# Queries projected transposed, and VectorE's 32x32 block transposes in place of TensorE's, in a linear-attention and gated-MLP layer

## The chip, the cores and the metric

The kernel runs on one core of one Trainium2 chip. The metric is the device time of one execution in microseconds (us). The engines are TensorE (PE in the profile, with its weight loads as PEld), VectorE (DVE), ScalarE (ACT), GpSimd (POOL) and SyncE (SP), which issues most DMAs. TensorE's granted clock was 1.00 over the whole profiled execution.

## What is computed

All numbers are float32. `x` has 2048 tokens of 512 features, there are 32 heads of 16 features, and the MLP is 1376 wide.

```python
xn = _layernorm(x)
q, k, v = split_heads(xn @ wqkv)                   # 32 heads of 16
pq, pk = q @ w_phi[h], k @ w_phi[h]                # per head
phi_q = concat(softmax(pq), softmax(-pq))          # 32 features per head
phi_k = concat(softmax(pk), softmax(-pk))
kv = phi_k^T v;  z = sum over tokens of phi_k      # per head
o = (phi_q kv) / (phi_q z + 1e-6)
s = o @ wo
g = silu(((xn W_gate) * (gate > 0) * (xn W_up)) W_down)
out = x + s * g
```

## The kernel before

Every product is made of three matmuls of float32r operands: high part by high part and the two mixed products (`mm3`, L188). `split` (L183) makes the two parts: ScalarE copies the high part, VectorE or GpSimd subtracts it for the low part.

The work has these stages:

1. *Token stage* (about 20 to 169 us). A loop over 16 tiles of 128 tokens (L910). The order alternates between two blocks of 512 tokens (`order`, L209: blocks 2 and 3 first, then 0 and 1). Each round normalizes a tile, turns it by four TensorE transposes (`turn`, L304) into the shared tile `XT` (or `a21` for one quarter of the odd tiles, L289), and projects keys, values and queries by 12 matmuls of 512 columns each (`project`, L346). `query` (L351) projects queries with the tokens on the partitions, copies the result to SBUF (`pqs`) and stores it in DRAM. The weights of keys and queries are first multiplied by `w_phi` (`fold`, L226). `features` makes phi_k, and `kv_products` accumulates kv in PSUM (`pkv`, 8 matmuls of 256 columns for each tile).
2. *MLP, in two halves* of 1024 tokens (L1042). For each of 11 slices of 128 MLP features, `gate_up` (L508) makes 7 groups of 6 matmuls of 512 columns (`pa` to `pd`), and `down` adds the down projection (`py`) for slices in chunks. The slices' weights are split in the first half (`f_prep`), one slice ahead, and stored in DRAM for the second.
3. *Queries*, beside the MLP. `q_pair` (L611) handles two tiles of 128 tokens: it loads `pq`, copies it to PSUM on ScalarE (`fetch`), takes maxima and minima, subtracts, applies exp, sums, weighs by z (`weigh`, on GpSimd, `zB` holds z for all 1024 columns) and normalizes; all with tokens on the partitions. `q_back` (L708) turns the normalized features `eq` by 16 TensorE transposes in four groups (`ppT`, L722), splits each group (`pTh` on ScalarE, `pTl` on VectorE, L723), and multiplies by kv (`pnum`, 16 matmuls of 256 columns). ScalarE copies the result to `o`, and four DMAs for each half store it (`o_store`). Pairs 0 to 2 belong to the first half, 3 to 7 to the second (`QUERIES`, L31).
4. *Output* after each half (L1104): `o_load` reads o (a load, and a GpSimd DMA that adds the second part), `o_split` splits it, `out_tile` (L781) makes 12 matmuls (`pso`), multiplies by the MLP's result, adds x and stores.

The order of instructions is fixed when the program is built. `Clock` (L56) is a planner: it keeps a modelled time for each engine (`FIXED` and `RATE` in cycles of TensorE, L59), and `pump` (L126), called between matmul groups, lets waiting jobs issue their next step when the model says that its inputs are ready and the engine is not too far behind. A step on TensorE or SyncE waits until its inputs have been ready for `MARGIN`, 3000 cycles. Each engine, and SyncE's queue, then runs its own list in that order.

```python
if key in ("tensor", "sync"):
    return all(self.there(x) + self.MARGIN <= self.now for x in tiles)
free = max(self.free[key], self.now)
return free - self.now <= self.LIMIT[key] * limit and all(self.there(x) <= free + 300 for x in tiles)
```

All engine instructions are recorded by one helper, so the profile gives L52 for them; the tiles' names tell them apart.

Of the kernel before, what the change touches and what calls it, by code (L numbers as in the profile page):

```python
# [13 lines left out]
P = 128  # L14
# [41 lines left out]
class Clock:  # L56
# [41 lines left out]
    def add(self, gen, after=0, limit=1):  # L98
        self.work.append([self.now + after * BT, (None,), gen, limit])
        return gen  # L100

    def later(self, after, op):
# [5 lines left out]
    def when(self, tile, op):  # L108
        def gen():
            yield "sync", tile  # L110
            op()
            yield None,
        self.add(gen())

    def due(self, at, wants, limit):
        key, *tiles = wants
# [32 lines left out]
def layer_kernel(ctx: ExitStack, tc: tile.TileContext, x, wkT, wqT, wv, wo, wf, cst, out):  # L149
# [52 lines left out]
    def flat(e):  # L202
        return e.rearrange("p h s f -> p (h s f)")
# [16 lines left out]
    def w_tile(name):  # L220
        return [(u2((P, D), f"{name}h", F32R), u2((P, D), f"{name}l", F32R)) for k in range(KD)]

    def rows(w):
        return lambda k: w[k]

    def fold(w, raw, k):  # L226

        p = ps(name="pfold")
        for j in range(KD):
            nc.tensor.matmul(p[:, j * P:(j + 1) * P], raw[:, j * P:(j + 1) * P], bd_sb[:, j, :],  # L230
                             start=True, stop=True)
        return lambda: split(*w[k], p)


    XT = sb.tile([P, 7, 2, 2, BT], F32R, tag="XT", name="XT")
    pace.shared = XT.name
    A21, XN, XF, SF = {}, {}, {}, {}

    def norm_stats(n):
        xt = X.pop(n)  # L240
# [43 lines left out]
    def xt_parts(n, s):  # L284

        if n % 2 == 0:
            return [(XT[:, A11:A12 + 1, s, :, cols(n)], slice(0, 2))]
        if n not in A21:
            A21[n] = u2((P, 2, 2, P), "a21", F32R)  # L289
        return [(A21[n][:, s], 0), (XT[:, A22, s, :, cols(n)], 1)]  # L290

    def hi_xt(n, p):
# [53 lines left out]
    def project(n, w, name):  # L346
        p = ps(name=name)
        mm3(p, xt_cols(n), rows(w), range(KD))
        return p

    def query(n):  # L351
        pq = project(n, WQ, "pq")
        t = u2((P, D), "pqs")
        nc.scalar.activation(t, pq, AF.Copy)
        b, i = order[n]
        PQ[b * TPB + i] = dram((P, D), f"pq{b * TPB + i}")
        pace.when(t, lambda: nc.sync.dma_start(PQ[b * TPB + i], t))

    def features(n, pk, pv, between):

# [239 lines left out]
            yield  # L600


    PQS, OD = {}, {}

    def q_load(q):
        for j in range(2):
            t = 2 * q + j
            PQS[t] = u2((P, D), "pql")
            nc.sync.dma_start(PQS[t], PQ[t])

    def q_pair(q):  # L611
        es = []
# [19 lines left out]

        def weigh(j):
            ez.append(u4((P, 1024), "ez"))
            nc.gpsimd.tensor_tensor(ez[j], flat(es[j]), zB, op=ALU.mult)

        def total(s, j):
            src = ez[j].rearrange("p (h f) -> p h f", f=DH) if s else groups(es[j])
# [6 lines left out]
        def expo(j):  # L645
            nc.scalar.activation(flat(es[j]), flat(es[j]), AF.Exp)

        yield "scalar", PQS[2 * q]
        fetch(0)
        yield "vector", pv[0]  # L650
        bounds(0)
        yield from step_of(q - 1, 2)
        yield "vector", pv[0]
        shift(0)
        yield "scalar", es[0], PQS[2 * q + 1]
        expo(0)
        fetch(1)
        yield "vector", pv[1]
        bounds(1)
        yield from step_of(q - 1, 4)  # L660
        yield "vector", pv[1]
        shift(1)
        if q + 1 < NP:
            q_load(q + 1)
# [5 lines left out]
        total(0, 0)  # L670
        yield "vector", es[1]
        total(0, 1)
        yield from step_of(q - 1, 5)
        yield "gpsimd", es[1]
        weigh(1)
        yield "vector", sums
# [15 lines left out]
        for j in range(2):  # L692
            yield "vector", r
            normalize(j)
        DONE_Q[q] = 0
        BACK[q] = pace.add(q_back(q, es))

    BACK, DONE_Q = {}, {}
# [9 lines left out]
    def q_back(q, es):  # L708


        OD[q] = dram((P, 4, 256), f"od{q}"), dram((P, 4, 256), f"ol{q}")
        ts = [(u4((P, 4, 256), "pTh", F32R), u4((P, 4, 256), "pTl", F32R)) for hf in range(2)]
        for j in range(2):
            for hf in range(2):
                th, tl = ts[hf]
                yield "vector", es[j]
                yield "tensor", es[j]
                ef = flat(es[j])
                p = ps((P, 4, P), name="ppT")
# [4 lines left out]
                if hf:  # L724
                    es[j] = None
                DONE_Q[q] += 1
        for hf in range(2):
            th, tl = ts[hf]
            yield "tensor", tl
            os_ = u4((P, 2, 2, 256), "o")  # L730
            for o in range(2):
                p = ps((P, 2, 256), name="pnum")
                for s in range(2):
                    g = 2 * o + s
                    mm(p[:, s, :], kvhl[:, 1, hf * 4 + g, :], th[:, g, :], True, False)
                    mm(p[:, s, :], kvhl[:, 0, hf * 4 + g, :], tl[:, g, :], False, True)
                nc.scalar.activation(os_[:, o], p, AF.Copy)
            ts[hf] = None
            DONE_Q[q] += 1
            pace.when(os_, lambda hf=hf, os_=os_: o_store(q, hf, os_))  # L740
        yield None,

    def o_store(q, hf, os_):

        for s in range(2):
            for part in range(2):
                r = slice(0, 64) if s == part else slice(64, P)
                to = slice(0, 64) if s == 0 else slice(64, P)
                nc.sync.dma_start(OD[q][part][to, 2 * hf:2 * hf + 2, :], os_[r, :, s, :])


    OHL, OF, SX, YK = {}, {}, {}, {}
# [53 lines left out]

    def wo_fetch(k):
        WR[k] = u2((P, D), "wor")
        nc.sync.dma_start(WR[k], wo[:, k, :])

    def wo_prep(k):
        raw, hi, lo = WR.pop(k), u2((P, D), "woh", F32R), u2((P, D), "wol", F32R)
# [43 lines left out]
    WK, WV, WQ = w_tile("wk"), w_tile("wv"), w_tile("wq")  # L856

    def wv_split(k):
        split(*WV[k], wv_raw[:, k, :], nc.gpsimd)
    norm_vector(0)  # L860
    folds = [fold(WK, wk_raw[:, k, :], k) for k in range(2)]
    norm_vector_apply(0)
# [110 lines left out]
    def state():  # L973
# [31 lines left out]
                low(g2 - 1)  # L1005
            yield "tensor", kvacc
        low(g2)
        zB = u4((P, 1024), "zB")
        for c in range(2):
            yield "tensor", zacc  # L1010
            p = ps(name="pz")
            nc.tensor.matmul(p, ones, flat(zacc)[:, c * 512:(c + 1) * 512], start=True, stop=True)
            nc.vector.tensor_copy(zB[:, c * 512:(c + 1) * 512], p)

    def all_queries(half):
        if not half:
# [25 lines left out]
    for half in range(2):  # L1042
        b0, b1 = 2 * half, 2 * half + 1
        for f in range(NF):
# [124 lines left out]
```

## Time and profile before

| | |
|---|---|
| time, median of 3 runs | 583.93 us (583.33 to 584.82) |
| the profiled execution's own time | 583.24 us |
| its span | 581.5 us |
| instructions | 8525 |
| busy: PE, DVE, ACT, POOL | 99%, 68%, 50%, 67% of the span |
| TensorE transposes of query features (`ppT`) | 128, 272 ns each |
| query projection (`pq`) | 192 matmuls of 128x512, about 390 ns each |
| numerators (`pnum`) | 128 matmuls of 128x256, about 280 ns each |
| DVE low parts (`pTl`) | 32 of 128x512, 690 ns each |
| POOL weighing (`ez`) | 16 of 128x1024, 2408 ns each |
| DMA | 138.26 MB, 238 GB/s on average |

The span runs from the first to the last instruction that the profiler recorded; the execution's own time is 1.7 us longer. In the profile's groups, a line names engine, operation, output<-inputs, shape and count, then the busy time of the group, the mean duration of one, and the idle time of the engine before them with what ended it. Matmuls overlap one another, so the duration of one is longer than its share of TensorE's time. The chain of waits follows the work that ended last back to its start, at each step to what released it. In the view of stretches, each engine has its busy time and, in brackets, its number of instructions.

### The profile page before, as it was taken

The page shows a single profiled execution, that of the slowest core. Times are in us where ns is not written, and L with a number is a line of the kernel's source. Part 1 is how long each engine was busy: PE and PEld are TensorE (multiplying, and loading weights), DVE is VectorE, ACT ScalarE, POOL GpSimd, SP SyncE. Part 2 cuts the span into 40 slices and gives each one's busy share as a digit, 9 for nine tenths or more (in the row PEclk, how much of TensorE's full clock was granted, in tenths as well). Part 3 has the DMA queues.
Part 4 walks back from the last instruction along what each step waited for, and adds up shares of the span by engine and source line. Part 5 has one row for each costly group of instructions (what it writes and reads, how often), then busy time and mean ns, then how long its engine had stood idle before and what let it go on. Part 6 is the DMA issues. An engine that isn't in the chain of part 4 may idle for free.

```text
span 581.5 us, 8525 instructions
## 1 busy us (share of the span) xinstructions
PE 575.2 (99%) x2786; PEld 480.2 (83%) x2786; DVE 395.6 (68%) x605; ACT 289.4 (50%) x529; POOL 390.1 (67%) x341
## 2 busy tenths in 40 slices
PE   8999999999999999999999999999999999999997
PEld 7788888888888888888888888888888888888886
DVE  4898777767648975888784532588888878673322
ACT  3998787854535358254244151144544545434510
POOL 1779988979875586997967342543557575775384
PEclk9999999999999999999999999999999999999999
DMA  8356999964698747888858999894676384769863
GB/s 309 128 173 173 270 291 264 296 183 100 194 262 298 287 149 234 288 290 285 274 201 260 330 392 397 314 388 161 162 252 167 128 248 151 194 206 276 247 176 114
DMA packets 82700, 138.26 MB, mean 238 GB/s; under 512 B 7648, under 2 KB 30560, under 8 KB 81760
## 3 DMA queue, kind: packets, MB, share of 16 engines
q1 hardware_dynamic: 79200, 125.60, 64.2%
q0 software_dynamic: 3312, 12.06, 10.8%
q8 instruction: 22, 0.36, 0.3%
q14 instruction: 22, 0.18, 0.1%
q10 hardware_dynamic: 144, 0.07, 0.0%
HBM read 77.14 MB, written 52.69 MB: 223 GB/s over the span
## 4 chain that ended last, share of the span: by engine, by line
PE 97%; DMA 1%; ACT 1%; DVE 1%; SPq 0%; issue 0%; POOL 0%; POOLq 0%
PE py L52 21%; PE pd L52 10%; PE pa L52 10%; PE pc L52 10%; PE pso L52 8%; PE pk L52 8%; PE pq L52 8%; PE pv L52 7%; PE pb L52 5%; PE pkv L52 3%; PE pnum L52 3%; PE ppT L52 2%; PE pxT L52 1%; PE pfold L52 1%; DMA wkT<-wkT 1%; PE pkb L52 0%
## 5 line engine op out<-in xcount | busy, mean ns | idle before, releaser
L52 PE MATMUL pa<-XT,wa 128*128 128x512 f32 x264 | 68.9, 393 | 0.0
L52 PE MATMUL py<-fdh,hl 128*128 128x512 f32 x176 | 68.8, 391 | 0.0
L52 PE MATMUL py<-fdh,hh 128*128 128x512 f32 x176 | 68.6, 390 | 0.0
L52 PE MATMUL py<-fdl,hh 128*128 128x512 f32 x176 | 68.5, 389 | 0.0
L52 POOL TENSOR_TENSOR hl<-e,hh 128x512 fp32r<-128x512 f32 x22 | 28.4, 1292 | 56.1 <-ACT hh L52 51.8
L52 PEld LDWEIGHTS pa<-XT,wa 128*128 128x128 f32 x264 | 48.5, 188 | 9.4
L52 ACT ACTIVATE hh<-e 128x512 fp32r<-128x512 f32 x22 | 13.9, 632 | 72.0 <-DVE e L52 65.0
L52 POOL TENSOR_TENSOR phl<-ek,phl 128x1024 fp32r<-128x1024 f32 x15 | 36.1, 2405 | 19.2 <-ACT phl L52 19.2
L52 POOL TENSOR_TENSOR hl<-u,hh 128x512 fp32r<-128x512 f32 x22 | 28.5, 1294 | 27.1 <-ACT hh L52 27.1
L52 DVE TENSOR_TENSOR y<-py,y 128x512 f32<-128x512 f32 x40 | 27.5, 689 | 27.2 <-PE py L52 27.1
L52 POOL TENSOR_TENSOR y<-y,ys 128x512 f32<-128x512 f32 x24 | 31.0, 1295 | 17.0 <-ACT ys L52 17.0
L52 PEld LDWEIGHTS py<-fdh,hh 128*128 128x128 f32 x176 | 33.0, 188 | 7.0
L52 PEld LDWEIGHTS py<-fdl,hh 128*128 128x128 f32 x176 | 33.1, 188 | 6.7
L52 PEld LDWEIGHTS py<-fdh,hl 128*128 128x128 f32 x176 | 33.0, 188 | 6.7
L52 POOL TENSOR_TENSOR ez<-eq,zB 128x1024 f32<-128x1024 f32 x16 | 38.5, 2408 | 0.0
L52 DVE TENSOR_TENSOR pTl<-ppT,pTh 128x512 fp32r<-128x512 f32 x32 | 22.1, 690 | 23.1 <-ACT pTh L52 22.7
L52 PE MATMUL pd<-XT,wd 128*128 128x512 f32 x132 | 35.0, 395 | 0.0
L52 POOL TENSOR_TENSOR ol<-of,oh 128x1024 fp32r<-128x1024 f32 x8 | 19.4, 2433 | 23.0 <-ACT oh L52 16.1
L52 PE MATMUL pd<-XT,wc 128*128 128x512 f32 x132 | 34.5, 392 | 0.0
L52 PE MATMUL pb<-XT,wb 128*128 128x512 f32 x132 | 34.5, 393 | 0.0
L52 PE MATMUL pc<-XT,wb 128*128 128x512 f32 x132 | 34.3, 391 | 0.0
L52 PE MATMUL pc<-XT,wc 128*128 128x512 f32 x132 | 34.1, 391 | 0.0
(166 smaller groups left out, 1637.6 us busy)
## 6 DMA issues: line engine op xcount, KB each, us to landing
zacc<-ek POOLq DMA_DIRECT2D x15, 512.0 KB, 5.2
xts<-XT SPq DMA_DIRECT2D x4, 1792.0 KB, 11.7
XT<-xts SPq DMA_DIRECT2D x7, 1024.0 KB, 14.9
wa<-ws SPq DMA_DIRECT2D x26, 256.0 KB, 5.3
wb<-ws SPq DMA_DIRECT2D x26, 256.0 KB, 5.2
wc<-ws SPq DMA_DIRECT2D x26, 256.0 KB, 5.3
rawg<-wf SPq DMA_DIRECT2D x22, 256.0 KB, 3.6
ws<-wa SPq DMA_DIRECT2D x22, 256.0 KB, 4.1
```

What stands on the lines that cost most here:

```text
L52: return self.tc.keep_in_program_order(op(*a, **k))
```

## The change

- *Projection.* `query` makes the queries with features on the partitions: the weights' slices of 128 columns are the stationary operand, two token tiles (256 columns) the moving one; 24 matmuls of 256 columns for each call instead of 12 of 512. The odd tiles' `a21` is shared by two tiles for that. The pair of tiles is the same that `q_pair` uses later.
- *To tokens.* `fetch` turns the loaded queries by a VectorE transpose of 32x32 blocks into PSUM, instead of ScalarE's copy. A partition then holds one of 32 tokens and one of four groups of features; the rest of both lies in the free dimension.
- *To features.* `q_back` turns `eq` by a VectorE block transpose into the tile of `ez`, instead of 16 TensorE transposes; ScalarE makes the high part of 1024 columns, and VectorE (pairs 0 to 2) or GpSimd (pairs 3 to 7) the low part. `pnum` reads its moving operand in runs of 32 columns. The result goes into the tile of `eq`.
- *Heads.* Keys, values and the rows of `wo` are taken with even heads first, by views where their weights are split or loaded. `zB` has 256 columns and is broadcast over the token blocks.
- *Order.* `q_back` goes to the front of the planner's list; the waits between pairs (`step_of`) are fewer; the second half's queries start after 5 matmul times instead of 30; an output tile's store waits until the planner holds it for ready, instead of 10 matmul times; `o_load` waits for the issue of its stores. There are 10 u4 buffers instead of 9 and 41 u2 instead of 44.

```diff
-B8, B4, B2 = 3, 9, 44
+B8, B4, B2 = 3, 10, 41
...
+        self.work.insert(0 if first else len(self.work), [self.now + after * BT, (None,), gen, limit])
...
+    def even_first(t):
+        return t.rearrange("p (m a f) -> p a m f", a=2, f=DH)
+    def by_parity(t):
+        return t.rearrange("p (a m f) -> p a m f", a=2, f=DH)
...
     def query(n):
-        pq = project(n, WQ, "pq")
-        t = u2((P, D), "pqs")
-        nc.scalar.activation(t, pq, AF.Copy)
...
+        b, h, j = order[n - n % 4 + n % 4 // 2][0], n // 4, n % 2
+        c = slice(h % 2 * 2 * P, (h % 2 + 1) * 2 * P)
...
+        p = ps((P, 2, 2 * P), name="pq")
+        for d in range(2):
+            w = slice((2 * j + d) * P, (2 * j + d + 1) * P)
+            mm3(p[:, d, :], lambda k: [t[:, w] for t in WQ[k]], x_of, range(KD))
...
         def fetch(j):
             pv.append(ps(name="pq2"))
-            nc.scalar.activation(pv[j], PQS.pop(2 * q + j), AF.Copy)
+            t = PQS.pop(2 * q + j)
+            nc.vector.transpose(pv[j], t.rearrange("p d t -> p (d t)"))
...
+            z = zB[:, 2 * j:2 * j + 2, :].unsqueeze(2).to_broadcast([P, 2, 8, 64])
...
-        BACK[q] = pace.add(q_back(q, es))
+        BACK[q] = pace.add(q_back(q, es, ez), first=True)
...
-                for g in range(4):
-                    c = (hf * 4 + g) * P
-                    transpose(p[:, g, :], ef[:, c:c + P])
-                split(th[:, :, j * P:(j + 1) * P], tl[:, :, j * P:(j + 1) * P], p)
...
+            et, ez[j] = ez[j], None
+            nc.vector.transpose(et, flat(es[j]))
...
+            nc.scalar.activation(th, et, AF.Copy)
+            lo = "vector" if q in QUERIES[0] else "gpsimd"
+            yield lo, th
+            add(getattr(nc, lo), tl, et, f32(th), ALU.subtract)
...
+            vh, vl = (t.rearrange("p (d t a x) -> p d a t x", d=2, a=2, x=32) for t in (th, tl))
...
+                    mm(o, kvhl[:, 1, g, :], vh[:, s, a], True, False)
+                    mm(o, kvhl[:, 0, g, :], vl[:, s, a], False, True)
...
     def o_load(q):
         pace.finish(BACK[q])
+        for g in STORES.pop(q):
+            pace.finish(g)
...
-            pace.later(10, lambda: nc.sync.dma_start(to, y))
+            pace.when(y, lambda: nc.sync.dma_start(to, y))
...
+        a, j = divmod(k, 2)
+        for s in range(2):
+            nc.sync.dma_start(WR[k][64 * s:64 * s + 64, :],
+                              wo[:, 2 * j + s, :].rearrange("(i a f) d -> a i f d", a=2, f=DH)[a])
...
-                queries = pace.add(all_queries(1), 30)
+                queries = pace.add(all_queries(1), 5)
```

More of the change, by code (lines that the diff above doesn't have):

```diff
@@ L96, in issued, with add @@
         self.ready[o.name] = self.free[key] + (380 if key == "tensor" else 0)
-    def add(self, gen, after=0, limit=1):
-        self.work.append([self.now + after * BT, (None,), gen, limit])
+    def add(self, gen, after=0, limit=1, first=False):
+        self.work.insert(0 if first else len(self.work), [self.now + after * BT, (None,), gen, limit])
         return gen
@@ L112, in gen @@
             yield None,
-        self.add(gen())
+        return self.add(gen())
     def due(self, at, wants, limit):
@@ L231, in fold @@
                              start=True, stop=True)
-        return lambda: split(*w[k], p)
+        if w is WQ:
+            return lambda: split(*w[k], p)
+        return lambda: split(*map(by_parity, w[k]), even_first(p))
     XT = sb.tile([P, 7, 2, 2, BT], F32R, tag="XT", name="XT")
     pace.shared = XT.name
-    A21, XN, XF, SF = {}, {}, {}, {}
+    A21, A21P, XN, XF, SF = {}, {}, {}, {}, {}
     def norm_stats(n):
@@ L288, in xt_parts @@
         if n not in A21:
-            A21[n] = u2((P, 2, 2, P), "a21", F32R)
+            if n % 4 == 1:
+                A21P[n // 4] = u4((P, 2, 2, 2 * P), "a21", F32R)
+            c = n // 2 % 2 * P
+            A21[n] = A21P[n // 4][:, :, :, c:c + P]
         return [(A21[n][:, s], 0), (XT[:, A22, s, :, cols(n)], 1)]
@@ L351, in query, with x_of @@
     def query(n):
-        pq = project(n, WQ, "pq")
-        t = u2((P, D), "pqs")
-        nc.scalar.activation(t, pq, AF.Copy)
-        b, i = order[n]
-        PQ[b * TPB + i] = dram((P, D), f"pq{b * TPB + i}")
-        pace.when(t, lambda: nc.sync.dma_start(PQ[b * TPB + i], t))
+        b, h, j = order[n - n % 4 + n % 4 // 2][0], n // 4, n % 2
+        c = slice(h % 2 * 2 * P, (h % 2 + 1) * 2 * P)
+        def x_of(k):
+            if n % 4 < 2:
+                return XT[:, k // 2, 0, k % 2, c], XT[:, k // 2, 1, k % 2, c]
+            if k // 2:
+                return XT[:, A22, 0, k % 2, c], XT[:, A22, 1, k % 2, c]
+            return A21P[h][:, 0, k, :], A21P[h][:, 1, k, :]
+        p = ps((P, 2, 2 * P), name="pq")
+        for d in range(2):
+            w = slice((2 * j + d) * P, (2 * j + d + 1) * P)
+            mm3(p[:, d, :], lambda k: [t[:, w] for t in WQ[k]], x_of, range(KD))
+        if n % 4 == 3:
+            A21P.pop(h)
+        t = u2((P, 2, 2 * P), "pqs")
+        nc.scalar.activation(t, p, AF.Copy)
+        q = 2 * b + h % 2
+        PQ[q, j] = dram((P, 2, 2 * P), f"pq{q}{j}")
+        pace.when(t, lambda: nc.sync.dma_start(PQ[q, j], t))
     def features(n, pk, pv, between):
@@ L606, in q_load @@
         for j in range(2):
-            t = 2 * q + j
-            PQS[t] = u2((P, D), "pql")
-            nc.sync.dma_start(PQS[t], PQ[t])
+            PQS[2 * q + j] = u2((P, 2, 2 * P), "pql")
+            nc.sync.dma_start(PQS[2 * q + j], PQ[q, j])
     def q_pair(q):
@@ L646, in expo @@
             nc.scalar.activation(flat(es[j]), flat(es[j]), AF.Exp)
-        yield "scalar", PQS[2 * q]
+        yield from step_of(q - 2, 4)
+        yield "vector", PQS[2 * q]
         fetch(0)
@@ L651, in q_pair @@
         bounds(0)
-        yield from step_of(q - 1, 2)
-        yield "vector", pv[0]
         shift(0)
-        yield "scalar", es[0], PQS[2 * q + 1]
+        yield "scalar", es[0]
         expo(0)
+        yield "vector", PQS[2 * q + 1]
         fetch(1)
@@ L659, in q_pair @@
         bounds(1)
-        yield from step_of(q - 1, 4)
-        yield "vector", pv[1]
         shift(1)
@@ L672, in q_pair @@
         total(0, 1)
-        yield from step_of(q - 1, 5)
         yield "gpsimd", es[1]
@@ L694, in q_pair @@
             normalize(j)
-        DONE_Q[q] = 0
-        BACK[q] = pace.add(q_back(q, es))
-    BACK, DONE_Q = {}, {}
+        DONE_Q[q], STORES[q] = 0, []
+        BACK[q] = pace.add(q_back(q, es, ez), first=True)
+    BACK, DONE_Q, STORES = {}, {}, {}
     def step_of(q, k):
@@ L706, in step_of, with q_back @@
                 yield 1,
-    def q_back(q, es):
+    def q_back(q, es, ez):
         OD[q] = dram((P, 4, 256), f"od{q}"), dram((P, 4, 256), f"ol{q}")
-        ts = [(u4((P, 4, 256), "pTh", F32R), u4((P, 4, 256), "pTl", F32R)) for hf in range(2)]
         for j in range(2):
[L714 to L719, printed above, removed]
-                for g in range(4):
-                    c = (hf * 4 + g) * P
-                    transpose(p[:, g, :], ef[:, c:c + P])
-                split(th[:, :, j * P:(j + 1) * P], tl[:, :, j * P:(j + 1) * P], p)
[L724 to L728, printed above, removed]
+            yield "vector", es[j]
+            et, ez[j] = ez[j], None
+            nc.vector.transpose(et, flat(es[j]))
+            DONE_Q[q] += 1
+            th, tl = u4((P, 1024), "pTh", F32R), u4((P, 1024), "pTl", F32R)
+            yield "scalar", et
+            nc.scalar.activation(th, et, AF.Copy)
+            lo = "vector" if q in QUERIES[0] else "gpsimd"
+            yield lo, th
+            add(getattr(nc, lo), tl, et, f32(th), ALU.subtract)
+            del et
@@ L729, in q_back @@
             yield "tensor", tl
-            os_ = u4((P, 2, 2, 256), "o")
-            for o in range(2):
+            os_ = flat(es[j]).rearrange("p (a s t) -> p a s t", a=2, s=2)
+            vh, vl = (t.rearrange("p (d t a x) -> p d a t x", d=2, a=2, x=32) for t in (th, tl))
+            for a in range(2):
                 p = ps((P, 2, 256), name="pnum")
                 for s in range(2):
[L734 to L737, printed above, removed]
@@ L738, in q_back @@
-            ts[hf] = None
+                    g = 4 * a + 2 * j + s
+                    o = p[:, s, :].rearrange("p (t x) -> p t x", x=32)
+                    mm(o, kvhl[:, 1, g, :], vh[:, s, a], True, False)
+                    mm(o, kvhl[:, 0, g, :], vl[:, s, a], False, True)
+                nc.scalar.activation(os_[:, a], p, AF.Copy)
+            es[j] = None
+            del th, tl, vh, vl
             DONE_Q[q] += 1
-            pace.when(os_, lambda hf=hf, os_=os_: o_store(q, hf, os_))
+            STORES[q].append(pace.when(os_, lambda j=j, os_=os_: o_store(q, j, os_)))
@@ L741, in q_back, with o_store @@
         yield None,
-    def o_store(q, hf, os_):
+    def o_store(q, j, os_):
         for s in range(2):
@@ L748, in o_store @@
                 to = slice(0, 64) if s == 0 else slice(64, P)
-                nc.sync.dma_start(OD[q][part][to, 2 * hf:2 * hf + 2, :], os_[r, :, s, :])
+                nc.sync.dma_start(OD[q][part][to, j:4:2, :], os_[r, :, s, :])
     OHL, OF, SX, YK = {}, {}, {}, {}
@@ L1007, in state @@
         low(g2)
-        zB = u4((P, 1024), "zB")
-        for c in range(2):
+        zB = small(256, "zB", 1).rearrange("p (d x) -> p d x", d=4)
+        for a in range(2):
             yield "tensor", zacc
-            p = ps(name="pz")
-            nc.tensor.matmul(p, ones, flat(zacc)[:, c * 512:(c + 1) * 512], start=True, stop=True)
-            nc.vector.tensor_copy(zB[:, c * 512:(c + 1) * 512], p)
+            p = ps((P, 4, 4, 32), name="pz")
+            nc.tensor.matmul(p.rearrange("p d i x -> p (d i x)"), ones, flat(zacc)[:, a * 512:(a + 1) * 512],
+                             start=True, stop=True)
+            for i in range(4):
+                r = slice(32 * i, 32 * i + 32)
+                nc.scalar.activation(zB[r, :, 32 * a:32 * a + 32], p[r, :, i, :], AF.Copy)
     def all_queries(half):
```

6 lines of the change are left out of this document (3 added, 3 removed).

## The prediction

> **What bounds the kernel now.** I read the page first: busy times, then the chain that ended last.
>
> ```profile
> span 581.5 us, 8525 instructions
> ...
> PE 575.2 (99%) x2786; PEld 480.2 (83%) x2786; DVE 395.6 (68%) x605; ACT 289.4 (50%) x529; POOL 390.1 (67%) x341
> ...
> PE 97%; DMA 1%; ACT 1%; DVE 1%; SPq 0%; issue 0%; POOL 0%; POOLq 0%
> ```
>
> The chain is TensorE's (PE) own list, one matmul after the other. The view of PE's waits asks whether anybody makes it wait:
>
> ```profile
> PE pidle L52 <- DVE mhalf L52: 1.1, 1, 1.1
> PE pfold L52 <- DMA wkT<-wkT: 0.9, 1, 0.9
> PE pv L52 <- POOL wvl L52: 0.5, 2, 0.3
> PE pxT L52 <- DVE lr L52: 0.2, 1, 0.2
> ```
>
> 2.7 us, all in the first 23 us. So what leaves PE's list leaves the time, one for one, as long as nobody new makes PE wait. What an instruction costs in that list is its pitch, not its duration. The chain between 208 and 228 us gives pitches:
>
> ```profile
> 212.13 1.37 PE py L52 x6
> 213.49 0.44 PE ppT L52 x4
> 213.93 1.39 PE pd L52 x6
> ```
>
> Six matmuls of 512 columns take 1.37 us (0.227 each) though one lasts 0.39; four transposes take 0.44, though one lasts 0.272.
>
> **The change, part by part** (own time of the profiled execution: 583.24 us, span 581.5).
>
> 1. *Transposes leave PE.* `ppT` is 128 instructions, 32 groups of four: 32 x 0.44 = 14.1 us. The piece behind a group takes 1.39 instead of 1.36 or 1.37 (pd above, also pb, pc): about 0.015 to 0.03 x 32, another 0.5. Together **-14.6**; without any of the slow start behind a group it would be 32 x 0.353 = 11.3 (three pitches of 0.108 and one short one of 0.028, read from the starts at 209.46).
>  The Trainium skill (TensorE: Matmul & The Clock Gate, Part 4: PE-mode transpose) gives about 275 ns for one such transpose in a kernel. The trace agrees as to the duration (272), but an estimate by that figure, 128 x 0.275 = 35 us for this part, is refuted by the pitch; the sum does not use it.
>
> 2. *Query projection.* 192 matmuls of 512 columns (43.7 us by pitch) become 384 of 256 columns, with twice the weight loads. The nearest row is `pkv`: 128x256, new weights each time, 128 of them in 15.1 us from start to start, 0.118 each. 384 x 0.1175 = 45.1: **+1.4**. Bounds: 0 (half of 0.227 each) and +28.5, if each weight load of 188 ns were paid in full (384 x 0.188 - 43.7); I take pkv, whose loads also last 188 and are hidden, and that speaks against the upper end so plainly that the range leaves it out. The pair of token tiles that a query now needs: for query(0) tile 2's low part on VectorE (DVE) ended at 26.4 us and pq began at 28.9, so 2.5 us of cover; later pairs have a whole round of 9.3 us.
>
> 3. *pnum* stays 128 matmuls of 256 columns (pitch 0.117), but reads its moving operand in runs of 32 columns. No row shows such a read. Bounds 0 and +14 (the pitch of 512 columns); I take 0, since what pnum shares with all rows is one column per pitch step.
>
> 4. *VectorE work.* Per query pair come two transposes of 512 and two of 1024 columns; four `pTl` of 0.69 go; for pairs 0 to 2 two low parts of 1024 come to DVE, for pairs 3 to 7 to GpSimd (POOL). No row shows a DVE transpose. Nearest are DVE operations of that size: 0.69 (`eq<-pq,mx`) and 1.21 (`eq<-eq,qr`); from below 0.55 (`xn` of 512 elements, all in SBUF), from above twice the size, 1.4 and 2.4. I take 0.69 and 1.21.
>  The stretches of the queries, before (busy columns PE, PEld, DVE, ACT, POOL):
>
> ```profile
> 195.00:309.00 114.00, 114.00 (x551) 95.37 (x550) 89.61 (x131) 52.59 (x101) 92.12 (x88) 1.00 0.72 237
> 375.00:533.00 158.00, 158.00 (x775) 132.24 (x774) 122.97 (x175) 77.74 (x132) 94.78 (x67) 1.00 0.68 215
> ```
>
>  First half: DVE +3 x 3.5 = 100 us in 114 - 12 x 0.44 = 108.7, 92% (from above, with transposes twice as long, 98%). POOL 92 of 108.7. Second half: DVE +5 x 1.0 = 128 in 149.2 (86%), POOL +10 x 2.41 = 119 (80%). All fit, the first half narrowly. ACT loses 9.4 (`pq<-pql`) and some of `pTh`: no cover needed. The weighing by a broadcast `zB` keeps 2.41; strided POOL rows of that size (`phl`, 2.405) show no surcharge; from above 3.1 (twice 1.54, `XT<-sa`), which is 16 x 0.7 on POOL.
>
> 5. *What is late next.* Before, DVE's normalizing released `ppT`, and `pTl` released `pnum`; the planner leaves 3000 of its cycles (1.25 us) ahead of a PE step, and in the trace the last pTl ended 1.0 to 2.2 us ahead of the second half's pnum (0.97 at 497.25, 1.43 at 227.24). After, three steps in a row stand there: DVE transpose, ACT high part, low part. They are modelled 3 to 9% short (1024 columns: DVE 1.09 against 1.13 pitch, ACT 0.87 against 0.95), 0.3 us in all. And the low part on DVE reads two SBUF tiles, which the kernel avoided so far for large tiles (its factor lies in PSUM). The few small ones show the price:
>
> ```profile
> 421.45 0.29 DVE L52 TENSOR_TENSOR qs<-qs,qr 128x128 f32<-128x128 f32 x1
> 421.77 1.32 DVE L52 SCALAR_TENSOR_TENSOR qd<-qs 128x64 f32<-128x64 f32 x1
> ```
> ```profile
> 421.72 1.29 POOL L52 TENSOR_TENSOR hl<-u,hh 128x512 fp32r<-128x512 f32 x1 [2.27 <-ACT hh L52]
> ```
>
>  `qd` takes 0.22 when POOL is idle and here 1.32, until POOL's instruction ends. So each of the six low parts of pairs 0 to 2 can wait 0 to 2.4 us for a POOL instruction, about 1.0 on average with POOL at 85%, and hold POOL 1.2 us itself. Against 1.0 to 1.6 of cover that leaves some 0.3 us of PE wait each, 1.8, and 0.3 for the ten POOL low parts: **+2.1** (bounds 0 and 16 groups x 1.5 = 24).
>  The Trainium skill (GPSIMD Engine Reference, section 8, Key points) states that GpSimd shares its SBUF interfaces with VectorE, in contention where a VectorE instruction has two SBUF inputs or a 2-port mode. The trace agrees (1.32 for 0.22). Whether a transpose from SBUF to SBUF falls under it, no run here shows.
>
> 6. *The last pair.* In the changed order the second half of pair 7's pnum stands 27 matmuls (6.1 us) ahead of the first `pso`, where before it stood in the last gate-and-up block. Behind it: ACT 1.1, four stores 2.6 and landing 2.4, load 3.6 (548.85 to 552.48), POOL accumulation behind yk, yk and ol (about 560.1 instead of 555.9), landing 7.6 (555.9 to 563.5), oh 1.05, ol 2.4: about 571.6, and tile 14 begins at 572.1. Cover 0.5; I take **+0.5** (bounds 0 and +4).
>
> 7. *The tail.* Stores of the output wait until the planner holds y for ready, no longer ten matmuls. Thus on SyncE's queue both half stores of tile 15 now stand ahead of those of tiles 12, 13 and 14, which before were issued earlier but for one between the halves:
>
> ```profile
> 577.40 1.72 SPq L52 DMA_DIRECT2D out<-y  x3
> ```
>
>  Three issues in 1.72 with waits; 577.40 and 577.83 stand back to back, 0.43 each; the 512-wide one landed 2.1 us after issue, the last half 1.7. Three more: 3 x 0.43 + 0.4 = **+1.7** (bounds 0 and 2.5).
>
> Nothing else moves PE: stores and loads of pq, the wo rows (two DMAs instead of one, four times) and zB are as long as before and off the chain; 10 u4 and 41 u2 buffers serve fewer live tiles per pair.
>
> Sum: 583.2 - 14.6 + 1.4 + 2.1 + 0.5 + 1.7 = 574.3 for the profiled execution. The median shown, 583.93, lies 0.7 above it: **575.0**.
>
> **The rivals.**
> - *All cover holds, and the tail does not grow*: without 2.1, 0.5 and 1.7 it is 570.0 + 0.7 = 570.7; with the tail 572.4. For it: DVE is below 93%. Against: the order of the stores is fixed in the program.
> - *The first half fills up*: transposes last twice as long or hold for POOL too. DVE at 98% plus six holds of 1.0 is 104%: some 4 to 8 us more of PE wait, 579 to 583.
> - *Slower*: pnum takes the wait. If each of the 16 groups has its low part 2.5 us late (the big transpose held like `xn`, which took 1.50 at 13.19 us under a POOL instruction instead of 0.55, and then the low part again, behind a weighing of 2.41), then 1.25 us of cover leave 1.25 x 16 = 20 in place of 2.1: 593. It decides from 11.0 us of waits on, 0.69 per group, where the gain is gone. Against: in pairs 3 to 7 no DVE operation of size has two SBUF tensors. (Point 3 at its upper end would give 589.)
> - *It doesn't do what it says*: the order lists have no ppT, 32 VectorE transposes and 384 pq. Excluded.
>
> **How the numbers follow.** Forecast with waits between 0 and 6 us (572 to 579): 0.62. Clean, below 572: 0.13. First half full, 579 to 582.2: 0.12. Around the old time, within 0.3% (1.75 us, about what a measurement can tell from no change): 0.06. Slower: 0.07. Faster: 0.87. The range leaves out what lies below 571 and above 582.
>
> **What would show it.** pnum groups without idle PE ahead of them and no ppT; pq at 0.117 pitch; PE's list ending near 567 to 569 on a span of about 572.5; the three stores behind the last half. PE waits on `pTl` name point 5, on `ol` point 6. I am wrong if DVE transposes last over 1.5 us, or if pnum's pitch is not 0.117.

## The result, and the profile after

The changed kernel takes 580.24 us (median of 4 runs, 579.74 to 580.39) against 583.63 (4 runs, 583.24 to 584.82). The ratio is 0.9937, 95% interval 0.992 to 0.9954. So it is faster, by 3.4 us (0.6%) and not by the 8.9 forecast. The profiled execution took 579.74 with a span of 578.0. Of all runs below, one (of e6, 587.02 us) came out in a slower state of the chip, and it is left out.

The page of the changed kernel, its busy times and the chain that ended last:

```profile
span 578.0 us, 8608 instructions
...
PE 566.1 (98%) x2850; PEld 477.9 (83%) x2850; DVE 409.3 (71%) x609; ACT 280.8 (49%) x505; POOL 417.4 (72%) x351
...
PE 50%; DMA 2%; DVE 0%; SPq 0%; issue 0%
PE py L52 17%; PE pso L52 8%; PE pa L52 7%; PE pc L52 7%; PE pd L52 7%; PE pb L52 3%; PE pnum L52 2%; DMA wa<-ws 2%; SPq L52 0%; DVE y L52 0%; DVE e L52 0%; DVE u L52 0%
```

PE is busy for 9.1 us less, but the span is only 3.5 shorter: PE now waits, and more time passes behind its last matmul. In the part of the run that the chain reaches back over (52% of the span), it is no longer PE alone: 2% lie with a DMA, the reload `wa<-ws`. The waits of PE, in the order of the view:

```profile
PE pv L52 <- ACT pqs L52: 1.9, 2, 1.5
PE pfold L52 <- DMA wkT<-wkT: 1.1, 1, 1.1
PE pidle L52 <- DVE mhalf L52: 1.1, 1, 1.1
PE pv L52 <- POOL wvl L52: 0.5, 2, 0.3
PE pa L52 <- DMA wa<-ws: 0.4, 1, 0.4
PE pxT L52 <- DVE lr L52: 0.2, 1, 0.2
PE pc L52 <- DVE e L52: 0.2, 1, 0.2
```

Three of these were not there before: `pv` behind ScalarE's copy `pqs`, `pa` behind the reload, `pc` behind VectorE. `pnum`, where the forecast put its new wait, is not among them.

A table by stage says more than the sum. Each stage runs from one landmark on PE to the next, in the profiled execution: to the second `pk`, to the first `pa`, to the first half's `pso`, to the second half's `pa`, to its `pso`, to the start of PE's last matmul, to the end. The runs e1 to e10 are the experiments below. In all of them the two output stages take 16.8 and 27.9 us, so these columns are left out.

| us | start | token stage | first half | second half | tail | span |
|---|---|---|---|---|---|---|
| before | 22.86 | 145.98 | 180.47 | 183.53 | 3.91 | 581.47 |
| after | 23.60 | 150.77 | 175.84 | 176.73 | 6.31 | 577.97 |
| e1 six token tiles ahead | 23.05 | 148.95 | 175.86 | 176.75 | 6.31 | 575.64 |
| e2 queries from 5 matmuls | 23.28 | 150.07 | 178.35 | 175.50 | 6.30 | 578.21 |
| e3 all output stores later | 23.57 | 150.48 | 175.86 | 180.02 | 4.12 | 578.76 |
| e4 transposes put back | 23.52 | 150.10 | 180.83 | 184.61 | 6.30 | 590.08 |
| e5 e1 and late tail stores | 23.25 | 148.87 | 175.86 | 177.90 | 4.13 | 574.72 |
| e6 e5 and queries from 12 | 22.65 | 148.90 | 180.46 | 175.55 | 4.12 | 576.40 |
| e7 kernel before, 41 buffers | 23.96 | 148.12 | 180.78 | 183.66 | 3.90 | 585.14 |
| e8 all low parts on POOL | 24.27 | 150.67 | 182.78 | 175.69 | 6.29 | 584.41 |
| e9 late tail stores alone | 24.47 | 150.10 | 175.86 | 177.01 | 4.13 | 576.29 |
| e10 e5 and stores behind reload | 23.32 | 148.95 | 175.84 | 175.66 | 4.12 | 572.61 |

From before to after, the halves gain 4.6 and 6.8. The token stage loses 4.8, the tail 2.4, the start 0.7. The start lies between 22.65 and 24.47 over these executions, whatever was changed, so its 0.7 is no effect of the change. Each row is one execution, and a stage differs between executions that have the same edits in it: the token stage by up to 0.7 us (after and e2), the second half by up to 1.2 (e1 and e5). Smaller steps in these two columns are no proof by themselves.

**The token stage.** Rounds without a stall take 9.77 us instead of 9.66 (fourth to fifth `pk`: 42.32 to 52.09, before 41.21 to 50.87). That is the new `pq`: 24 steps of 0.119 instead of 12 of 0.227. 16 x 0.11 = 1.8. Most of the other 3.0 comes in three rounds. The longest stall, on ScalarE and then on PE:

```profile
111.69 0.60 ACT L52 ACTIVATE vhl<-pv 128x512 fp32r<-128x512 f32 x1 [1.54 <-DMA zacc<-ek]
112.18 0.62 ACT L52 ACTIVATE ek<-ek 128x512 f32<-128x512 f32 x1
115.87 0.60 ACT L52 ACTIVATE pqs<-pq 128x512 f32<-128x512 f32 x1 [3.07 <-POOL wc L52]
```
```profile
114.47 0.60 PE L52 MATMUL pxT<-ident,xn 128*128 128x128 f32 x4
116.52 0.50 PE L52 MATMUL pv<-wvh,XT 128*128 128x512 f32 x1 [1.46 <-ACT pqs L52]
```

`pqs` does not read `wc`, yet it starts just as POOL's `wc` ends (115.84). By the program, that instruction is the last to read a 2 KB buffer (the high part of `wc`), and `pqs` needs one to write to. So I read it as a wait for a buffer, which e1 and e7 put to the test: ScalarE waits 3.07 us for a place to put the result, `pq` stays in its PSUM bank, and the next `pv` waits 1.46 us for that bank. ScalarE's waits of this kind in the token stage were one of 1.3 us before (`pqs` on `wa`), and are 3.1, 2.8 and, on a 4 KB buffer, 1.5 (`vhl` on `zacc<-ek`) after.

**The second half's start.** SyncE's queue, first of before, then of after; its columns are start, length, and what is issued:

```profile
360.62 0.96 SPq L52 DMA_DIRECT2D sx<-x  x2
363.36 5.33 SPq L52 DMA_DIRECT2D out<-y  x5
368.78 0.87 SPq L52 DMA_DIRECT2D wa<-ws  x2
```
```profile
366.24 1.01 SPq L52 DMA_DIRECT2D sx<-x  x2
368.98 4.09 SPq L52 DMA_DIRECT2D out<-y  x4
373.16 0.88 SPq L52 DMA_DIRECT2D wa<-ws  x2
```

The second half begins at 366.1 and 367.0. The reload for its second slice was issued 2.7 us after that, and now 6.2 after it; it landed at 377.35, and PE had stood for 0.4 us by then. This goes back to pair 2: its numerators began at 310.8 and 317.9 instead of 304.6 and 307.6, and everything behind its stores on the queue (load of o, wo, `XT`, the first slice's reload, `sx`) is some 4 to 9 us later.

**The tail.** The queue's end, four in a row where before three stood (577.40):

```profile
572.88 1.80 SPq L52 DMA_DIRECT2D out<-y  x4
```

The last half store is the first of these four; the stores of tiles 12 to 14 stand behind it.

### The profile page after: what moved, and what is told of

The parts are those of the page before. It is cut to its first block, busy times and chain, and to the rows that moved or that the text cites. A ratio compares the mean times of both kernels' runs of the same rounds, so it can differ in the third digit from the quotient of the medians.

```text
span 578.0 us, 8608 instructions
## 1 busy us (share of the span) xinstructions
PE 566.1 (98%) x2850; PEld 477.9 (83%) x2850; DVE 409.3 (71%) x609; ACT 280.8 (49%) x505; POOL 417.4 (72%) x351
## 4 chain that ended last, share of the span: by engine, by line
PE 50%; DMA 2%; DVE 0%; SPq 0%; issue 0%
PE py L52 17%; PE pso L52 8%; PE pa L52 7%; PE pc L52 7%; PE pd L52 7%; PE pb L52 3%; PE pnum L52 2%; DMA wa<-ws 2%; SPq L52 0%; DVE y L52 0%; DVE e L52 0%; DVE u L52 0%
## 5 line engine op out<-in xcount | busy, mean ns | idle before, releaser
L52 PE MATMUL pa<-XT,wa 128*128 128x512 f32 x264 | 67.6, 391 | 0.5 <-DMA wa<-ws 0.4
L52 PEld LDWEIGHTS pa<-XT,wa 128*128 128x128 f32 x264 | 49.1, 188 | 11.5 <-DMA wa<-ws 1.4
L52 PE MATMUL pq<-XT,wqh 128*128 128x256 f32 x192 | 35.5, 283 | 0.0
L52 PE MATMUL pc<-XT,wc 128*128 128x512 f32 x132 | 35.3, 394 | 0.2 <-DVE e L52 0.2
L52 PE MATMUL pv<-wvh,XT 128*128 128x512 f32 x96 | 33.1, 399 | 1.9 <-ACT pqs L52 1.9
```

The costliest lines, as they stand in the source:

```text
L52: return self.tc.keep_in_program_order(op(*a, **k))
```

## Experiments

Ratios are to the kernel before, with 95% intervals.

**e4: the transposes put back, unread.** In `q_back`, ahead of each half's VectorE transpose:

```diff
+            for hf in range(2):
+                yield "tensor", es[j]
+                p = ps((P, 4, P), name="ppT")
+                for g in range(4):
+                    c = (hf * 4 + g) * P
+                    transpose(p[:, g, :], flat(es[j])[:, c:c + P])
+                del p
```

> Each half of a query pair gets its two groups of four TensorE transposes back, into a PSUM tile that nobody reads: 32 groups more on TensorE, everything else as in the changed kernel; the output is unchanged. Theory (step 1 of the sum, 0.44 a group and 0.5 behind them): +14 to +15, 594 to 595 in all, as the query blocks have no slack on TensorE. Rival (a group costs three pitches and a short one, 0.353): +11.3, 591.5. Second rival (the transposes lay beside waits that the changed kernel now has): +12 or less with stalls of TensorE in the query stages gone.

Measured: 591.78 us, ratio 1.0137 (1.0119 to 1.0154), 11.5 more than the changed kernel. Two groups now stand together:

```profile
213.69 1.03 PE L52 MATMUL ppT<-ident,eq 128*128 128x128 f32 x8
214.48 0.71 PE L52 MATMUL pb<-XT,wb 128*128 128x512 f32 x2
```

Eight transposes take 0.79 from start to start, and the first steps behind them are about 0.10 us longer together: 0.445 a group, 14.2 us for 32. The two halves grow by 5.0 and 7.9, so 1.3 of the 14.2 come back in them; PE's waits on `wa<-ws` and on `pc`, 0.6 in all, are gone, as PE comes later to both, and the rest was not taken apart. So the theory holds for the price and the second rival for the sum: the transposes cost what step 1 took for them, and waits hide a small part. The first rival's 11.3 lies close to the sum, but its price of 0.353 leaves out the slower steps that the trace shows behind each group.

**e1: one 2 KB buffer less in use.**

```diff
-        if n + 7 < N:
-            load_x(n + 7)
+        if n + 6 < N:
+            load_x(n + 6)
```
(and `range(3, 6)` for the first loads)

> One token tile less is loaded ahead (six instead of seven), which frees one of the 41 buffers of 2 KB; the matmuls are those of the changed kernel. Theory (buffers): in the changed kernel TensorE's token stage, from the second pk to the first pa, takes 150.8 us against 146.0 before, of which 2.0 is the pitch of the new pq (24 x 0.1185 against 12 x 0.2275, 16 times) and some 2.6 are three stalls (74.7, 91.8, 114.8 us) behind ScalarE's copy pqs<-pq and the split vhl<-pv, which wait for a free buffer (3.07, 2.79 and 1.54 us). With one buffer more the waits for 2 KB buffers go, so the stage takes about 148.5 and the run 578. Rival (the stage is longer by its matmuls alone, or its engines are late by work and not by buffers): 150.8 stays, 580.2.

Measured: 577.83, ratio 0.9896 (0.9879 to 0.9913); the token stage takes 148.95. The buffer theory holds in the main: the same matmuls take 1.8 us less when a token tile is loaded one round later (between 1.1 and 1.9, as e1, e5, e6 and e10 lie at 148.87 to 148.95, and the executions with the changed kernel's token stage at 150.07 to 150.77). But not all waits went, as the theory had it. Of the 3.0 lost beside the pitch, 1.2 stay, and 1.0 of that is in one round, where ScalarE's `pqs` still waits 3.29 us for the end of POOL's `wc` (113.46) and `pv` 0.78 us for `pqs`.

**e7: the old kernel with the new number of 2 KB buffers.**

```diff
-B8, B4, B2 = 3, 9, 44
+B8, B4, B2 = 3, 9, 41
```

> The kernel before the change with 41 buffers of 2 KB instead of 44, nothing else. Theory (it is the number of 2 KB buffers, not the new projection, that stalls the changed kernel's token stage): the old kernel keeps its a21 in these buffers, so it feels the three buffers at least as much as the changed kernel, whose token stage lost 2.6 us: +2 to +6 us, 586 to 590, with ScalarE or SyncE waiting for buffers between 60 and 165 us. Rival (the stalls come of the new projection, which holds its operands for two tiles and copies later, or of the 4 KB buffers): the old kernel stays at 584.

Measured: 586.26, ratio 1.0042 (1.0025 to 1.0058). The token stage takes 148.12 instead of 145.98, with a single stall, the same `pv` behind `pqs`:

```profile
PE pv L52 <- ACT pqs L52: 1.9, 1, 1.9
```

So three buffers fewer cost the old projection 2.1 us as well. The second half stays at 183.66: in the old kernel the number of these buffers does not make the reload late.

**e2: the first half's queries earlier.**

```diff
-                    queries = pace.add(all_queries(0), 20)
+                    queries = pace.add(all_queries(0), 5)
```

> The first half's query pairs may start after 5 instead of 20 matmuls of the first gate-and-up block; nothing else changes. Theory (SyncE's queue): pair 2's numerators came 6.2 and 10.3 us later in the changed kernel (310.8 and 317.9 against 304.6 and 307.6), so its stores, its load back, the wo rows and the x rows went out later, and the reload of wa<-ws landed 0.4 us after TensorE asked for it and some 1.9 us were lost in the first blocks of the second half (372 to 387 us). Fifteen matmuls are 3.4 us: pair 2 comes by about that much earlier and a part of the 1.9 goes, about 579 in all. Rival (DVE sets the pace of the first half's queries, 92% busy, so a start 3.4 us earlier is gone by pair 2, or the reloads are late by the share of the DMA engines alone): the wait on wa stays, 580.2.

Measured: 580.62 (single runs from 579.69 to 587.03), ratio 0.9959 (0.9936 to 0.9982). Pair 2's numerators begin at 297.3 and 304.4, `sx` goes out 9.4 us ahead of the second half (after 4.9, before 9.6), the wait on `wa` is gone and the second half takes 1.2 less. But the first half takes 2.5 more:

```profile
PE pc L52 <- DVE e L52: 1.7, 2, 1.4
```

Both theories are half right: pair 2's lateness does make the reload late, and VectorE has no room for an earlier start in the first blocks. In the sum the one offsets the other: the time cannot be told from the changed kernel's.

**e3 and e9: the stores of the output tiles later again,** all of them (e3), or those of tiles 12 to 14 alone (e9, by the edit shown at e5):

```diff
-            pace.when(y, lambda: nc.sync.dma_start(to, y))
+            pace.later(10, lambda: nc.sync.dma_start(to, y))
```

> The stores of the output tiles are issued ten matmuls later again, as before the change, instead of when the planner holds y for ready; nothing else changes. Theory: from the end of TensorE's list to the end of the span the changed kernel takes 6.3 us against 3.9 before, since three stores stand behind the last half store; this goes back to 3.9, so 580.2 - 2.4 = 577.8. At the start of the second half the stores of tiles 8 to 13 move as well and may take some tenths off the wait on wa<-ws. Rival (the end is as late because the last landings share the DMA engines, whatever their order): 580.2.

> The changed kernel with one edit: the stores of tiles 12, 13 and 14 go out ten matmuls later again; those of the other tiles stay as the change has them. Theory (the last term of the sum, by itself): 6.31 us from TensorE's last matmul to the end become 4.1, and nothing else moves, as no store at the start of the second half is touched: 580.2 - 2.2 = 578.0. Rival (the end is bound by the last landings): 580.2.

Measured: e3 580.18, ratio 0.9932 (0.9916 to 0.9949); e9 577.91, ratio 0.9903 (0.9882 to 0.9924). The tail is 4.12 and 4.13, so three stores behind the last half store cost 2.2 us, and e9 keeps that gain. In e3 it was lost at the start of the second half, and I had not expected that:

```profile
369.04 5.34 SPq L52 DMA_DIRECT2D out<-y  x5
374.47 0.88 SPq L52 DMA_DIRECT2D wa<-ws  x2
```
```profile
375.15 1.52 PE L52 MATMUL pd<-XT,wd 128*128 128x512 f32 x6
379.20 2.56 PE L52 MATMUL pa<-XT,wa 128*128 128x512 f32 x6 [2.54 <-DMA wa<-ws]
381.56 2.25 PE L52 MATMUL pb<-XT,wb 128*128 128x512 f32 x6
```

Five stores stand ahead of the reload instead of four, it goes out 1.3 us later, and PE waits 2.54. Then six matmuls take 2.56 and 2.25 where they take 1.52: the wait has let the clock down (last section). Second half: 180.02 instead of 176.73.

**e5: six tiles ahead (e1's edit), and the late stores of tiles 12 to 14:**

```diff
+            if t < 12:
+                pace.when(y, lambda: nc.sync.dma_start(to, y))
+            else:
+                pace.later(10, lambda: nc.sync.dma_start(to, y))
```

> Two edits on the changed kernel: six token tiles ahead instead of seven (577.83 by itself), and the stores of tiles 12, 13 and 14 ten matmuls later again, as before the change, while the stores at the start of the second half stay as the change has them. Theory (what was gained at the end with all stores moved, 6.31 to 4.12 us from TensorE's last matmul to the end of the span, was lost again at the start of the second half, where a fifth store came ahead of the reload of wa<-ws and TensorE waited 2.5 us for it): here only the gain is left, 577.8 - 2.2 = 575.6. Rival (the end takes as long, or the wait on wa grows for another reason): 577.8 or more.

Measured: 575.95, ratio 0.9862 (0.9839 to 0.9886). The two gains add up. In its profiled execution PE waits for the reloads, and the second half takes 177.90, 2.2 more than in e10 below:

```profile
PE pb L52 <- DMA wb<-ws: 1.0, 1, 1.0
...
PE pa L52 <- DMA wa<-ws: 0.7, 1, 0.7
```

**e6: e5 with the first half's queries from 12 matmuls** (`all_queries(0), 12`).

> As the run before it, and the first half's query pairs may start after 12 matmuls of the first gate-and-up block (20 in the changed kernel, 5 in the run that moved them alone). Theory: pair 2 comes early enough that SyncE's queue reaches the reload of wa<-ws in time, which takes away the 0.8 us wait at 374 us and some of the 0.3 us beside it, while VectorE is not yet overfull in the first blocks: 574.5 to 575. Rival (VectorE is overfull with any earlier start; starting after 5, pc waited 1.6 us for VectorE's e and pnum 0.3): 576 to 578.

Measured: 577.86 (576.53 to 579.34, five runs), ratio 0.9894 (0.9874 to 0.9914). The rival holds: in the profiled execution, the slowest of the five, the second half takes 175.55, but the first 180.46, with 1.94 us of wait for VectorE's `e` at 193 us and a slow clock behind it.

**e10: e5 with the output stores behind the reload.** The six stores of the first half wait 50 matmuls:

```diff
-            if t < 12:
+            if 6 <= t < 12:
                 pace.when(y, lambda: nc.sync.dma_start(to, y))
             else:
-                pace.later(10, lambda: nc.sync.dma_start(to, y))
+                pace.later(10 if t > 6 else 50, lambda: nc.sync.dma_start(to, y))
```

> As the run with six token tiles ahead and the late stores of tiles 12 to 14 (575.95), and the six output stores at the start of the second half wait 50 matmuls instead of for y alone, so that two instead of four of them stand ahead of the reload of wa<-ws on SyncE's queue. Theory (a place in SyncE's queue makes this reload late: each store ahead of it waits 1.25 us for GpSimd's y): the reload is issued 2.5 us earlier, TensorE's waits on wa and wb at 374 and 377 us (0.9 and 1.1) go, 574.0. Rival (the share of the DMA engines, 0.95 to 1.02 busy there, makes it late, whatever the order): the waits stay within 0.5 us, 575.5 to 576.5.

Measured: 574.96, ratio 0.9865 (0.9837 to 0.9893). The queue of e10:

```profile
366.88 1.59 SPq L52 DMA_DIRECT2D out<-y  x2
368.57 0.87 SPq L52 DMA_DIRECT2D wa<-ws  x2
369.53 0.86 SPq L52 DMA_DIRECT2D wb<-ws  x2
```

and its chain and PE's waits after the start:

```profile
PE 53%; DVE 0%; issue 0%
```
```profile
PE pv L52 <- ACT pqs L52: 0.7, 1, 0.7
...
PE pc L52 <- DVE e L52: 0.2, 1, 0.2
```

No wait on `wa` or `wb` is left, and no DMA in the chain. The theory holds against the share of the DMA engines: from 370 to 372 us, while e5's queue stood at the stores, they were only 0.50 busy, and in e10, where the reloads are out by then, 0.83. What it is worth depends on the execution: the second half takes 175.50 to 175.69 us in the four where PE does not wait for `wa` or `wb` (e2, e6, e8, e10), and 176.73 to 177.90 in after, e1, e5 and e9, where it does. In the median the step from e5 is 1.0 us and the intervals overlap; the profile shows it, not the timing. e10 beats both kernels: its interval lies below that of the changed kernel.

**e8: all low parts on POOL.**

```diff
-            lo = "vector" if q in QUERIES[0] else "gpsimd"
+            lo = "gpsimd"
```

> All 16 low parts pTl go to GpSimd; the changed kernel gives the six of the first half to VectorE. Nothing else changes. Theory A (step 5: a VectorE operation with two inputs in SBUF waits for GpSimd's instruction; the six took 1.39 us at the median where 1.13 is the least): VectorE gains 8 us, GpSimd gets 6 x 2.41 = 14.5 more on the 97 of 115 us that it has between 195 and 310, so it is full, low parts stand behind other work, pair 2 comes later yet and the waits at pnum and on wa<-ws grow: 581 to 584. Theory B (VectorE was what made pair 2 late): pair 2's numerators come earlier than 310.8 and 317.9, and the waits at the start of the second half shrink: 578.5 to 580.

Measured: 584.51, ratio 1.0003 (0.9988 to 1.0017). Theory A holds. The last pair of the first half:

```profile
325.63 0.39 PE L52 MATMUL pnum<-pTh,kvhl 128*128 128x256 f32 x1 [2.05 <-ACT pTh L52]
328.04 0.58 PE L52 MATMUL pnum<-pTl,kvhl 128*128 128x256 f32 x1 [2.03 <-POOL pTl L52]
...
329.71 2.76 PE L52 MATMUL pa<-XT,wa 128*128 128x512 f32 x6
```

Two waits of 2 us at `pnum`, and 6.8 us at half the clock behind them: the first half takes 182.78, 6.9 more. Six instructions on another engine cost the whole gain of the change. This is the mechanism of the slower rival, reached in one pair where the rival had it in 16 groups, and through POOL's load, not VectorE's holds.

## Why the prediction was wrong in size, point by point

The direction was right. The time was 5.2 us off in the median (580.24 for 575.0), and the step that failed is the sentence ahead of the sum: "Nothing else moves PE: stores and loads of pq, the wo rows (two DMAs instead of one, four times) and zB are as long as before and off the chain; 10 u4 and 41 u2 buffers serve fewer live tiles per pair." Both parts of it fell. Of the 5.4 us between the 574.3 of the sum and the profiled 579.74, the token stage has 3.4, the halves 1.1, the tail 0.7 and the start, by chance, 0.7; the 0.5 for the last pair did not come.

- *Buffers* (`u2` has 2 KB, `u4` 4 KB for each partition). They were counted for a query pair. The token stage uses the same buffers, with `pqs`, `xt`, `xn`, `xf`, `sa`, `sb` and the first slices' weights in them; it was not counted. It lost 3.0 us beside the pitch (e1 gives 1.8 of them back, e7 takes 2.1 from the old kernel). Nearly all that stays in e1 is behind the one wait of `pqs` that it leaves. `vhl`'s wait for a 4 KB buffer, where the `a21` pairs now lie, fell from 1.54 to 0.61 us there; whether ten of these are too few was not tried.
- *The queue.* The forecast followed the last pair of the second half to the end (step 6), but not pair 2, the last of the first half, whose stores head a long list on SyncE's queue. Of the 2.3 us by which the second half misses 20 x 0.456 = 9.1, e10 gives 1.1 back; the rest was not taken apart.
- *Step 1, -14.6*: right. e4 puts 0.445 on a group, 14.2 in all.
- *Step 2, +1.4*: right in mechanism; `pq` steps at 0.119 and not 0.1175, and the rounds grew by 1.8 in all. The weight loads of 188 ns stay hidden.
- *Step 3, 0*: `pnum` steps at 0.121 against 0.117, 128 x 0.004 = +0.5. The prediction named another pitch than 0.117 as a sign that it is wrong; what was sized wrong is this half microsecond. Whether it is the runs of 32 columns was not tested apart.
- *Step 4*: right as to the values taken. The transposes last what was taken. VectorE is less full than forecast in the first half (95.3 of 109 us, 87%, for 92%) and in the second (83% for 86%); POOL is at 88% for 85% and at 76% for 80%. The upper bound was added wrong: with transposes twice as long VectorE would have had 89.6 + 3 x 7.3 = 111 of 108.7 us, 102% and not 98%, and the second rival 108% and not 104%. It stood on transposes of 1.4 and 2.4 us, which did not come:

```profile
L52 DVE STREAM_TRANSPOSE ez<-eq 128x1024 f32<-128x1024 f32 x16 | 19.7, 1234 | 0.0
L52 DVE STREAM_TRANSPOSE pq<-pql 128x512 f32<-128x512 f32 x16 | 11.3, 706 | 0.0
L52 DVE TENSOR_TENSOR pTl<-ez,pTh 128x1024 fp32r<-128x1024 f32 x6 | 8.6, 1426 | 0.5 <-ACT pTh L52 0.5
```
```profile
200.00:309.00 109.00, 108.83 (x495) 90.31 (x494) 95.33 (x133) 48.41 (x90) 95.39 (x88) 1.00 0.73 248
375.00:527.00 152.00, 151.45 (x696) 125.24 (x695) 125.48 (x170) 67.73 (x107) 115.62 (x77) 1.00 0.73 233
```

- *Step 5, +2.1*: too much. PE waits 0.15 us at `pnum` in all. The hold by POOL is real, but POOL's instructions are short: the six low parts last 1.21 to 1.73, 8.6 in all, 1.3 above six of the shortest, so 0.2 on average and not 1.0. In its place VectorE made `pc` wait 0.33 us at 268 us. That the halves as a whole come out within 1.1 us of the forecast is in part luck: they gain 11.4 where steps 1, 3 and 5 together gave 12.5, but the 2.1 set down for `pnum` was lost elsewhere, at the reloads and in places that were not taken apart.
- *Step 6, +0.5*: nothing; PE does not wait for the last pair.
- *Step 7, +1.7*: 2.4, of which e9 shows 2.2. The term was sized by the queue alone. That part is right: 1.80 for four issues instead of 0.33 for one, 1.5. But from the end of the last issue to the end of the span it now takes 3.3 us (574.68 to 577.97) and before 2.35 (579.12 to 581.47), as the last transfer is a whole tile behind three others (that this is why was not tested apart).

With the two leaks mended in part and the tail in full, e10's profiled execution takes 574.38 and PE's last matmul starts at 568.5, in the 567 to 569 that the forecast named for the changed kernel, where it is 571.7. That this is the forecast's time is no proof of its sum, as e10 is another kernel. The steps that were worked out on PE's own list were right; the ones that were waved off were not.

## What to carry to other kernels

- When a change takes buffers from one pool and gives them to another, count the live tiles in every stage that draws on the pool, not only where the change is; an engine that waits for a place to write shows as a wait on whoever frees it (`pqs <- POOL wc`).
- Where one queue issues most transfers in a fixed order, a step that ends later moves all that stands behind it: follow the last such step of each stage to the next stage's first reload, and try moving a store that waits (1.25 us each here) behind the load that PE needs.

## What the hardware showed that was not expected

- *A wait of 1.9 us can halve TensorE's clock.* In e6 PE waited 1.94 us and in e3 2.54; the granted clock then stood at 0.5 for 3.41 us each time, and in e8, after 2.05 and 2.03 in a row, for 6.83. 512 columns then step at 0.427 instead of 0.227, so 3.41 us lose about 1.6 more. Waits of 1.87 us (e7) and 1.46 (after) did not do it. Nor does it come in every run of a kernel: of e6's five runs, the two of 579.0 and 579.3 us had a mean granted clock of 0.997, and the three of 576.5 to 577.9 one of 0.999 or 1.000, too high for such a stretch, which takes 0.003 off the mean. The view of windows of e3 (columns PE, PEld, DVE, ACT, POOL, clock, DMA share, GB/s):

```profile
376.30:379.00 2.70, 0.37 (x2) 0.00 (x0) 2.48 (x4) 0.63 (x1) 0.68 (x1) 1.00 1.01 307
379.00:382.80 3.80, 3.60 (x9) 2.84 (x10) 0.00 (x0) 1.00 (x2) 0.59 (x1) 0.59 1.04 396
```

 The Trainium skill (TensorE: Matmul & The Clock Gate, Part 1) has the clock halved after at least one idle window of about 3.4 us. The length of the slow stretch agrees (3.41), the wait that starts it was shorter here.
- *A VectorE transpose of 32x32 blocks from SBUF to SBUF is not held by POOL.* All 16 of 1024 columns lasted 1.23 or 1.24, the six of the first half with POOL 88% busy, while three of the six low parts, with two inputs in SBUF, waited for POOL's instruction, as this one:

```profile
268.59 1.73 DVE L52 TENSOR_TENSOR pTl<-ez,pTh 128x1024 fp32r<-128x1024 f32 x1
```
```profile
267.96 1.28 POOL L52 TENSOR_TENSOR wc<-tab,wc 128x512 fp32r<-128x512 f32 x1
269.21 1.72 POOL L52 TENSOR_TENSOR wd<-rawg,wd 128x256 fp32r<-128x256 f32 x1
```

 POOL's `wc` ends at 269.24, and the low part 1.08 after that, as the other two end 1.08 after a POOL instruction; POOL's next instruction starts beside it and takes 1.72. The prediction had left open whether the transpose would be held.
